# A gated decode block on one core: the whole kernel recorded into one critical section, with a loop on TensorE alone

## The chip, the cores and the metric

The kernel runs on one core of a Trainium2 chip. The metric is the device time of one execution in microseconds (us), lower is better; the time of a kernel is the median over its runs. A core has TensorE (PE; its weight loads are listed as PEld), VectorE (DVE), ScalarE (ACT), GpSimd (POOL) and SyncE (SP), each with an instruction queue of its own, and 16 DMA engines that move data between the chip's memory (HBM) and the core's SBUF.

## The reference, cut to what matters

```python
x = A_x                                     # (4, 1, 512), bf16
mod = silu(c) @ w_mod                       # six parts: sa, ca, ga, sb, cb, gb
h = layernorm(x) * (1 + ca) + sa
q = (h @ wq) as 32 heads of 128             # k_cache, v_cache: (4, 32, 4096, 128)
o = softmax(q . k_cache * 128**-0.5) . v_cache
x = x + ga * (o @ wo)
h = layernorm(x) * (1 + cb) + sb
z = gelu(h @ w_in); z1, z2 = halves of 896
g = w_sp * layernorm(z2) + b_sp             # S is 1: two scalars
out = x + gb * ((z1 * g) @ w_out)
```

The two caches have 134 MB each. They are read once; everything else is small.

## The kernel before, in words

The work is cut into 32 quads. A quad is one batch entry `b` and one group `g` of four heads; quad `i` is `(g, b) = (i // 4, i % 4)`. Its K is one 4 MB load into one of two buffers named `kt` (128 partitions, four heads by 32 parts of the sequence), its V another into one of two named `vt`; both are issued by SP, in the order K of the next quad, `wo_g` (the 512 KB of the output weights of a group, at the first quad of each group), V of this quad (lines 429 to 446). An issue waits until the buffer it writes is free. A load carries 32 KB packets, eight on each of the 16 DMA engines. Ahead of the quads SP loads `w_mod` and `wq` into the two `vt` buffers; the last K and V are cut into parts, and `wo_l`, `win` and `wout` follow them.

For each quad:

- `scores(i, half)`: VectorE multiplies half of K by the query in place (L276); TensorE then adds up the products, 16 matmuls against the identity `ident`, into `s_ps` (L281).
- `fold` (L290) adds eight columns; `softmax` takes the maximum over a head, ScalarE the exponentials (L311), VectorE writes them masked by head into `P4` (L314).
- `values(i - 1)`: 32 matmuls of `P4` with V (L341), and `zsum` the sums of the exponentials; ScalarE copies the result to `osb` (L347).
- `diagonal(i - 2)` picks the right head's rows with `sel` (L354, float32), `project(i - 2)` divides by the sums into `oT` (L375).
- `apply(i - 2)`, at the fourth quad of a group: 16 small matmuls rearrange `oT` (L391), VectorE copies to `oP` (L397), and 16 matmuls with `wo_g` add to `attn_ps` (L400).

In iteration `i` TensorE does diagonal, both halves of scores, values and apply, in this order. Before the loop over quads stand the modulation, the first layernorm and the queries `qbc` (L215 to L266); behind it the second layernorm, the gated MLP and the output (L474 to L545). The whole program is unrolled on all five engines. The order on each engine is that of the text (`tc.manual_schedule()`); the framework (Tile) allots buffers and semaphores and places the waits. Probabilities `P4` and maxima `mx` have three buffers, `wo_g`, `oT` and `oP` two.

Of the kernel before, what the change touches and what calls it, by code (L numbers as in the profile page):

```python
# [8 lines left out]
BF16 = mybir.dt.bfloat16  # L9
# [3 lines left out]
AX = mybir.AxisListType  # L13


@with_exitstack
def kernel(
# [16 lines left out]
    nc = tc.nc  # L34
    ctx.enter_context(tc.manual_schedule())
# [12 lines left out]
    EL = HT * DH  # L48
    DC = 8
    assert J == 4 and DH == P and SK % R == 0 and HT * DC == 512 and FH % P == 0  # L50
    att_scale = float(DH) ** -0.5
    LN_EPS = 1e-5

    consts = ctx.enter_context(tc.tile_pool(name="consts", bufs=1))
    persist = ctx.enter_context(tc.tile_pool(name="persist", bufs=1))
    kvp = ctx.enter_context(tc.tile_pool(name="kv", bufs=1))
    wk = ctx.enter_context(tc.tile_pool(name="work", bufs=1))

    rows = persist.tile([2 * B, D], BF16, name="rows")
    nc.scalar.dma_start(out=rows[0:B], in_=c)
    nc.scalar.dma_start(out=rows[B:2 * B], in_=A_x.rearrange("b s d -> (b s) d"))
    nc.scalar.preload_act_table_set("natural_log_exp_and_others")
    wb_t = persist.tile([1, 2], BF16, name="wb_t")
    nc.gpsimd.dma_start(out=wb_t[:, 0:1], in_=B_w_sp[0:1, 0:1])
    nc.gpsimd.dma_start(out=wb_t[:, 1:2], in_=B_b_sp.rearrange("(a b) -> a b", b=1))


    def vslot(cols):  # L70
        return kvp.tile([P, cols], BF16, name="vt", bufs=2)

    wm = vslot(J * 6 * D)
    nc.sync.dma_start(out=wm, in_=w_mod.rearrange("(p j) n -> p (j n)", j=J))
    wm = wm.rearrange("p (j n) -> p j n", j=J)
    GW = NH * DH
    wq = vslot(J * G * GW)
    nc.sync.dma_start(out=wq, in_=A_wq.rearrange("(p j) n -> p (j n)", j=J))  # L78
    wq = wq.rearrange("p (j n) -> p j n", j=J)

    quads = [(g, b) for g in range(G) for b in range(B)]

    def kv_view(cache, i):
        g, b = quads[i]
        return cache[b, g * NH:(g + 1) * NH].rearrange("h (s n) d -> (h s) (n d)", s=R)

    def load(cache, i, tag, parts):
        t = kvp.tile([P, NT * DH], BF16, name=tag, bufs=2)
        a = 0
        for part in parts:  # L90
            b = a + NT * DH // part
            nc.sync.dma_start(out=t[:, a:b], in_=kv_view(cache, i)[:, a:b])  # L92
            a = b
        return t.rearrange("p (n d) -> p n d", d=DH)

    def load_k(i):
        return load(A_k_cache, i, "kt", (2, 2) if i == len(quads) - 1 else (1,))

    def load_v(i):
        return load(A_v_cache, i, "vt", (2, 4, 8, 16, 16) if i == len(quads) - 1 else (1,))  # L100

    NQ = len(quads)


    ident = consts.tile([P, P], BF16, name="ident")
    make_identity(nc, ident)
    ones_b = consts.tile([1, P], BF16, name="ones_b")
    nc.vector.memset(ones_b, 1.0)
    ones_f = consts.tile([P, P], F32, name="ones_f")
    nc.vector.memset(ones_f, 1.0)  # L110

    sel = consts.tile([P, 32], F32, name="sel")
    nc.vector.tensor_reduce(
        out=sel, in_=ident.rearrange("p (t m) -> p m t", m=32), axis=AX.X, op=ALU.add,
    )
    mean_d = consts.tile([P, P], F32, name="mean_d")
    nc.vector.memset(mean_d, 1.0 / D)
    mean_f = consts.tile([P, P], F32, name="mean_f")
    nc.vector.memset(mean_f, 1.0 / FH)
    eps = consts.tile([P, 1], F32, name="eps")  # L120
    nc.vector.memset(eps, LN_EPS)
    wide = consts.tile([P, 4 * P], BF16, name="wide")
    nc.gpsimd.memset(wide, 0.0)
    busy_ps = [None]

    def keep_busy(n):

        if busy_ps[0] is None:
            busy_ps[0] = psum_s.tile([P, 4 * P], F32, name="big", bufs=2)
        for _ in range(n):  # L130
            nc.tensor.matmul(busy_ps[0], lhsT=ident, rhs=wide, start=True, stop=True)

    NB = 3

    mask4 = consts.tile([P, NH], F32, name="mask4")
    nc.gpsimd.memset(mask4, 0.0)
    for hl in range(NH):
        nc.gpsimd.memset(mask4[hl * R:(hl + 1) * R, hl:hl + 1], 1.0)
    P4s, mxs = [], []
    for i in range(NB):  # L140
        t = consts.tile([P, NT + 4, NH], BF16, name=f"P4_{i}")
        nc.gpsimd.memset(t, 0.0)
        P4s.append(t)
        t = consts.tile([P, R], F32, name=f"mx_{i}")
        nc.gpsimd.memset(t, 0.0)
        mxs.append(t)
# [4 lines left out]
    def ln_stats(pool, psum, buf, ones, n, name, meanwhile=None):  # L151

        nc.vector.tensor_tensor(out=buf[:, 1], in0=buf[:, 0], in1=buf[:, 0], op=ALU.mult)
        ps = psum.tile([P, 2, n, B], F32, name="small", bufs=1)
        nc.tensor.matmul(
            ps.rearrange("p s j b -> p (s j b)"), lhsT=ones,
            rhs=buf.rearrange("p s j b -> p (s j b)"), start=True, stop=True,
        )
        if meanwhile is not None:
            meanwhile()  # L160
        st = pool.tile([P, 2, B], F32, name=f"st_{name}")
        nc.vector.tensor_reduce(
            out=st, in_=ps.rearrange("p s j b -> p s b j"), axis=AX.X, op=ALU.add,
        )
        msq = pool.tile([P, B], F32, name=f"msq_{name}")
        nc.vector.tensor_tensor(out=msq, in0=st[:, 0], in1=st[:, 0], op=ALU.mult)
        var = pool.tile([P, B], F32, name=f"var_{name}")
        nc.vector.tensor_tensor(out=var, in0=st[:, 1], in1=msq, op=ALU.subtract)
        rstd = pool.tile([P, B], F32, name=f"rstd_{name}")
        nc.scalar.activation(out=rstd, in_=var, func=AF.Ln, bias=eps)  # L170
        nc.scalar.activation(out=rstd, in_=rstd, func=AF.Exp, scale=-0.5)
        return st[:, 0], rstd


    modT = persist.tile([P, 6, J, B], F32, name="modT")
    qbc = persist.tile([P, B, G, DH], BF16, name="qbc")
    x1b = persist.tile([P, 2, J, B], F32, name="x1b")
    wbf = persist.tile([P, 2], F32, name="wbf")
    xcT = persist.tile([P, J, 2 * B], F32, name="xcT")
    cT, x4T = xcT[:, :, 0:B], xcT[:, :, B:2 * B]  # L180
    xT = persist.tile([P, J, B], F32, name="xT")


    gwb = persist.tile([P, J, 3, B], F32, name="gwb")
    sT = persist.tile([P, J, B], BF16, name="sT")
    hbc = persist.tile([P, J, B, R], BF16, name="hbc")
    psum_acc = ctx.enter_context(
        tc.tile_pool(name="psum_acc", bufs=1, space=bass.MemoryType.PSUM)
    )
    attn_ps = psum_acc.tile([P, J, B], F32, name="attn_ps")  # L190
    psum_s = ctx.enter_context(
        tc.tile_pool(name="psum_s", bufs=1, space=bass.MemoryType.PSUM)
    )

    def mod_part(oc):
        ps = psum_s.tile([P, J, B], F32, name="small", bufs=1)
        for jo in range(J):
            c0 = oc * D + (jo if oc < 2 else jo * P)
            cols = slice(c0, c0 + (P - 1) * J + 1, J) if oc < 2 else slice(c0, c0 + P)
            for j in range(J):  # L200
                nc.tensor.matmul(
                    ps[:, jo, :], lhsT=wm[:, j, cols],
                    rhs=sT[:, j, :], start=(j == 0), stop=(j == J - 1),
                )
        if oc in (1, 4):
            nc.vector.tensor_scalar_add(out=modT[:, oc], in0=ps, scalar1=1.0)
        else:
            nc.vector.tensor_copy(out=modT[:, oc], in_=ps)

    def query(b, g0, n, qp):  # L210

        for j in range(J):
            wv = wq[:, j, :].rearrange("p (g h d) -> p g h d", h=NH, d=DH)
            for hl in range(NH):
                nc.tensor.matmul(  # L215
                    qp[hl * R:(hl + 1) * R, 0:n], lhsT=hbc[:, j, b, :],
                    rhs=wv[:, g0:g0 + n, hl, :],
                    start=(j == 0), stop=(j == J - 1),
                    tile_position=(0, hl * R),
                )  # L220

    with tc.tile_pool(name="pre", bufs=1) as pre:
        xc_ps = psum_s.tile([P, J, 2 * B], F32, name="small", bufs=1)
        for j in range(J):
            nc.tensor.matmul(
                xc_ps[:, j, :], lhsT=rows[:, j::J],
                rhs=ident[0:2 * B, 0:2 * B], start=True, stop=True,
            )
# [24 lines left out]
        for oc in range(2, 6):  # L253
            mod_part(oc)
# [321 lines left out]
```

## Time and profile before

| | before |
|---|---|
| median of 3 runs | 667.79 us (667.62 to 667.85) |
| span of the profiled execution (first to last instruction) | 665.5 us; the page lists no other time for it |
| PE, DVE, ACT, POOL busy | 415.7, 402.6, 41.3, 4.7 us |
| PE instructions | 3024 weight loads and 3024 matmuls |
| moved from HBM | 282.73 MB, 425 GB/s over the span |
| granted TensorE clock, mean | 0.771 |
| scores matmul L281, VectorE product L276 | 457 ns x1024, 4420 ns x64 |
| K, V: issue to landing, median | 26.0, 33.7 us |

In the profile's slices the span is cut into 40 equal parts of 16.6 us, and a digit gives tenths of a part in which an engine was busy (9: 90% or more). A DMA queue is a stream of packets from one source: q1 holds the loads that SP issues, q8 packets of TensorE's program. A row of instructions gives line, engine, operation, destination and sources, the size of the operation and how often it ran; a figure in brackets behind `<-` is the idle time before it and what ended that.

### The profile page before, as it was taken

What the parts mean: (1) busy time and instruction counts of PE and PEld (TensorE: products, weight loads), DVE (VectorE), ACT (ScalarE), POOL (GpSimd) and SP (SyncE); (2) the same over time, 40 slices, a digit from 0 to 9 for tenths busy, and PEclk for the clock granted to TensorE, in tenths of its full rate; (3) what the DMA queues carried; (4) which work ended last, traced back from release to release, by engine and by line L of the source; (5) the groups of instructions that cost most, each with busy time, mean ns of one, the idle gap of its engine ahead of it and who ended that gap; (6) DMA issues with size and microseconds to landing.
All of it is one profiled execution on the core that took longest, in us unless ns stands there. A gap on an engine that the chain in (4) does not pass through costs nothing.

```text
span 665.5 us, 6939 instructions
## 1 busy us (share of the span) xinstructions
PE 415.7 (62%) x3024; PEld 204.6 (31%) x3024; DVE 402.6 (61%) x475; ACT 41.3 (6%) x115; POOL 4.7 (1%) x21
## 2 busy tenths in 40 slices
PE   2557776655677655676555477654657655657775
PEld 2223333222333322233222233232223322223334
DVE  2166776675556576547666456666555666655762
ACT  1200000000000000000000000000000000000002
POOL 2000000000000000000000000000000000000000
PEclk9977777668887667887667788676888766888795
DMA  9999999999999999999999999999999999999995
GB/s 379 439 425 427 437 439 424 429 438 434 427 428 441 428 428 434 435 426 434 433 436 424 436 435 430 423 439 435 428 431 435 433 430 432 437 426 435 428 417 236
DMA packets 12749, 283.17 MB, mean 426 GB/s; under 512 B 1448, under 2 KB 1968, under 8 KB 4016
## 3 DMA queue, kind: packets, MB, share of 16 engines
q1 hardware_dynamic: 12640, 282.73, 98.9%
q8 instruction: 23, 0.38, 0.2%
q14 instruction: 6, 0.05, 0.0%
q0 software_dynamic: 64, 0.00, 0.0%
q10 hardware_dynamic: 16, 0.01, 0.0%
HBM read 282.73 MB, written 0.00 MB: 425 GB/s over the span
## 4 chain that ended last, share of the span: by engine, by line
DMA 62%; PE 24%; DVE 12%; issue 0%; SPq 0%; ACT 0%; DVEq 0%
DMA kt<-in_A_k_cache_dram 58%; PE s_ps L281 24%; DVE kt L276 11%; DMA vt<-in_A_v_cache_dram 3%; DMA wout_437<-in_B_w_out_dram 1%; PE big L341 0%; DVE S L290 0%; ACT E L311 0%; SPq L92 0%; DVE P_1_109 L314 0%; DVE P_0_105 L314 0%; PE y_ps L522 0%; DVE nm L308 0%; DVE mT L300 0%; SPq L78 0%
## 5 line engine op out<-in xcount | busy, mean ns | idle before, releaser
L281 PE MATMUL s_ps<-kt,ident 128*128 128x512 bf16 x1024 | 293.5, 457 | 185.5 <-DVE kt L276 185.5
L276 DVE TENSOR_TENSOR kt<-kt,qbc 128x8192 bf16<-128x8192 bf16 x64 | 282.7, 4420 | 82.9 <-DMA kt<-in_A_k_cache_dram 82.9
L281 PEld LDWEIGHTS <-ident 128*128 128x128 bf16 x1024 | 116.4, 114 | 351.1 <-issue 229.8
L290 DVE TENSOR_REDUCE S<-s_ps 128x64 f32<-128x512 f32 x64 | 44.3, 692 | 125.5 <-PE s_ps L281 125.5
L354 PE MATMUL zo_ps<-sel,osb 128*128 128x4 f32 x248 | 33.2, 257 | 26.6 <-ACT osb L347 26.6
L311 ACT ACTIVATE E<-S,nm 128x128 f32<-128x128 f32 x32 | 12.8, 401 | 563.4 <-DVE nm L308 563.4
L354 PEld LDWEIGHTS zo_ps<-sel,osb 128*128 128x128 f32 x248 | 30.6, 194 | 38.4 <-ACT osb L347 38.4
L341 PE MATMUL big<-vt,P_0_105 128*32 128x512 bf16 x352 | 21.0, 380 | 1.5 <-DMA vt<-in_A_v_cache_dram 1.5
L341 PE MATMUL big<-vt,P_1_109 128*32 128x512 bf16 x320 | 19.1, 380 | 0.0
L341 PE MATMUL big<-vt,P_2_113 128*32 128x512 bf16 x320 | 19.1, 380 | 0.0
L347 ACT COPY osb<-big 128x512 f32<-128x512 f32 x31 | 17.6, 566 | 20.0 <-PE big L341 20.0
L215 PE MATMUL big<-vt,hbc 128*32 128x512 bf16 x128 | 9.6, 471 | 5.2 <-DMA vt<-in_A_wq_dram 5.2
L314 DVE TENSOR_TENSOR P_1_109<-E,mask_99 128x512 bf16<-128x512 f32 x11 | 7.6, 692 | 6.8 <-ACT E L311 6.8
L314 DVE TENSOR_TENSOR P_0_105<-E,mask_99 128x512 bf16<-128x512 f32 x11 | 7.6, 692 | 6.7 <-ACT E L311 6.7
L341 PEld LDWEIGHTS <-P_0_105 128*32 128x32 bf16 x352 | 8.4, 96 | 8.9 <-DMA vt<-in_A_v_cache_dram 1.6
L314 DVE TENSOR_TENSOR P_2_113<-E,mask_99 128x512 bf16<-128x512 f32 x10 | 6.9, 692 | 6.2 <-ACT E L311 6.2
L400 PE MATMUL attn_ps<-oP,wo_g 128*128 128x4 bf16 x112 | 3.8, 164 | 10.6 <-DVE oP L397 10.6
L341 PEld LDWEIGHTS <-P_1_109 128*32 128x32 bf16 x320 | 7.6, 96 | 6.7
L341 PEld LDWEIGHTS <-P_2_113 128*32 128x32 bf16 x320 | 7.6, 96 | 6.7
L375 DVE TENSOR_TENSOR oT<-zo_ps,rz 128x4 bf16<-128x4 f32 x32 | 5.4, 168 | 7.1 <-PE zo_ps L363 6.0
L215 PEld LDWEIGHTS <-hbc 128*32 128x32 bf16 x128 | 4.4, 114 | 10.3 <-issue 8.4
L308 DVE STREAM_TRANSPOSE nm<-hb 128x32 f32<-128x32 f32 x32 | 6.8, 212 | 1.1
(221 smaller groups left out, 131.1 us busy)
## 6 DMA issues: line engine op xcount, KB each, us to landing
kt<-in_A_k_cache_dram SPq DMA_DIRECT2D x31, 4096.0 KB, 26.0
vt<-in_A_v_cache_dram SPq DMA_DIRECT2D x31, 4096.0 KB, 33.7
vt<-in_A_wq_dram SPq DMA_DIRECT2D x1, 4096.0 KB, 20.4
kt<-in_A_k_cache_dram SPq DMA_DIRECT2D x2, 2048.0 KB, 24.8
wo_g<-in_A_wo_dram SPq DMA_DIRECT2D x7, 512.0 KB, 26.5
vt<-in_w_mod_dram SPq DMA_DIRECT2D x1, 3072.0 KB, 9.8
vt<-in_A_v_cache_dram SPq DMA_DIRECT2D x1, 2048.0 KB, 17.8
win_434<-in_B_w_in_dram SPq DMA_DIRECT2D x1, 1344.0 KB
```

What stands on the lines that cost most here:

```text
L215: nc.tensor.matmul(qp[hl * R:(hl + 1) * R, 0:n], lhsT=hbc[:, j, b, :], rhs=wv[:, g0:g0 + n, hl, :], start=(j == 0), stop=(j == J - 1), til ...
L276: nc.vector.tensor_tensor(out=kt, in0=kt, in1=q[:, None, :].to_broadcast([P, HT, DH]), op=ALU.mult,)
L281: nc.tensor.matmul(ps, lhsT=ident, rhs=kt[:, :, cc * DC:(cc + 1) * DC], start=(cc == 0), stop=(cc == DH // DC - 1),)
L290: nc.vector.tensor_reduce(out=st["S", i][:, half * HT:(half + 1) * HT], in_=st.pop(("s", i, half)), axis=AX.X, op=ALU.add,)
L308: nc.vector.transpose(out=nm, in_=hb)
L311: nc.scalar.activation(out=E, in_=S, func=AF.Exp, bias=nm[:, 0:1], scale=att_scale, accum_out=rs,)
L314: nc.vector.tensor_tensor(out=P4[:, 0:NT, :], in0=E[:, :, None].to_broadcast([P, NT, NH]), in1=mask4[:, None, :].to_broadcast([P, NT, NH]) ...
L341: nc.tensor.matmul(po[32 * t:32 * t + 32], lhsT=P4[:, n0:n0 + 8, :], rhs=st["v", i][:, n0:n0 + 4, :], start=(u == 0), stop=(u == NU - 1), ...
L347: nc.scalar.copy(out=osb, in_=po)
L354: nc.tensor.matmul(st["o", i], lhsT=osb[:, n, :], rhs=sel[:, NH * n:NH * n + NH], start=(n == 0), stop=(n == 3),)
L375: nc.vector.tensor_tensor(out=oT[:, :, b], in0=st.pop(("o", i)), in1=rz, op=ALU.mult,)
L400: nc.tensor.matmul(attn_ps[:, jo, :], lhsT=(wo_g[:, hl] if g < G - 1 else wo_l[hl // 2][:, hl % 2])[:, jo * P:(jo + 1) * P], rhs=oT[:, hl, :],
```

## The change: what it does

- The kernel no longer leaves waits and semaphores to Tile. Each operation is recorded in a `Program` with the regions it reads and writes; `order` finds, for each, which operations of other engines (and which loads) it must wait for, and leaves out those that an earlier wait covers. `run` then emits all engines' instructions inside one `tc.tile_critical()`.
- TensorE's part of quads 2 to 29 is emitted once, for four quads, inside `pe.Fori(0, 7)`; all other engines are still unrolled. What the loop waits for has semaphores of its own (`pe_...`), which TensorE lowers by the pass's count at the end of each pass.
- So that passes are alike, all buffers go by `i % 2`: `P4`, `mx` and the score tiles have two buffers, `wo_g`, `oT` and `oP` one. `wo_g` is loaded at the third quad of a group, between K and V. `attn_ps` is cleared by a matmul with zeros ahead of the loop, and all its matmuls add.
- Outside the tail a matmul is one recorded instruction that brings its weights along (`mm`); in the tail those with `wo_l`, `win` and `wout` are a weight load and a matmul with waits of their own (`mm2`). A semaphore is raised only by operations marked `done`.
- The two one-element loads of `w_sp` and `b_sp` go out from ScalarE's queue instead of GpSimd's; the identity is made by two recorded instructions.

```diff
+class Program:
...
+    def run(self, alloc, passes, engines):
+        self.order()
...
+        for name, lst in self.by_eng.items():
+            if name != "PE":
+                for op in lst:
...
+                    emit(op, engines[name], plain(op))
+        pe = engines["PE"]
+        seen = [o for o in self.by_eng["PE"] if o.passno is None]
+        first = loops[0][0].pos
+        for op in seen:
+            if op.pos < first:
+                emit(op, pe, plain(op))
+        with pe.Fori(0, passes):
+            for op, w in zip(loops[0], norm):
+                emit(op, pe, w.items())
+            for s in sorted(own):
+                if step[s]:
+                    pe.sem_inc(sems[s], -step[s])
+        for op in seen:
+            if op.pos > first:
+                emit(op, pe, [(s, v - passes * step.get(s, 0)) for s, v in plain(op)])
...
-    ctx.enter_context(tc.manual_schedule())
...
-        t = kvp.tile([P, NT * DH], BF16, name=tag, bufs=2)
...
+    kt = tile2([P, NT * DH], BF16, "kt")
+    vt = tile2([P, NT * DH], BF16, "vt")
...
-    NB = 3
+    P4s = tile2([P, NT + 4, NH], BF16, "P4_")
+    mxs = tile2([P, R], F32, "mx_")
...
+    wo_g = sb.tile([P, NH, D], BF16, name="wo_g")
...
+    def mm(out, lhsT, rhs, start, stop, done=False, **kw):
+        prog.add(
+            "PE", lambda e: e.matmul(out, lhsT=lhsT, rhs=rhs, start=start, stop=stop, **kw),
+            [lhsT, rhs], [out], done=done,
+        )
+    def mm2(out, lhsT, rhs, start, stop, done=False):
+        prog.add("PE", lambda e: e.ldweights(lhsT), [lhsT], [], done=False)
+        moving(out, lhsT, rhs, start, stop, done)
...
+    mm(cut(attn_b, J * B), ident, wide[:, 0:J * B], True, True, skip_group_check=True)
...
+    PASSES = (NQ - 4) // B
...
     for i in range(NQ):
+        prog.passno = (i - 2) // B if 2 <= i < 2 + B * PASSES else None
+        g, b = divmod(i, B)
         if i + 1 < NQ:
-            st["k", i + 1] = load_k(i + 1)
-        if quads[i][1] == 0:
-            g = quads[i][0]
-            if g < G - 1:
-                st["wo", g] = wk.tile([P, NH, D], BF16, name="wo_g", bufs=2)
-                nc.sync.dma_start(out=st["wo", g], in_=wo_w[g])
-        st["v", i] = load_v(i)
+            load_k(i + 1)
+        if b == 2 and g < G - 1:
+            load_sp("pe_wo", wo_g, wo_w[g])
+        load_v(i)
...
+    with tc.tile_critical():
+        sems = {}
+        def alloc(name):
+            sems[name] = tc.alloc_semaphore(name)
+            return sems[name]
+        prog.run(alloc, PASSES, {
+            "PE": nc.tensor, "DVE": nc.vector, "ACT": nc.scalar, "POOL": nc.gpsimd, "SP": nc.sync,
+        })
+        nc.sync.wait_ge(sems["out"], 16)
```

## The prediction

> **What bounds the kernel now.** I read the slices of the page first, then the queues, the chain, the windows at the end, the timeline, and last the trace's own list of DMA packets.
>
> ```profile
> PE   2557776655677655676555477654657655657775
> DMA  9999999999999999999999999999999999999995
> q1 hardware_dynamic: 12640, 282.73, 98.9%
> q8 instruction: 23, 0.38, 0.2%
> DMA 62%; PE 24%; DVE 12%; issue 0%; SPq 0%; ACT 0%; DVEq 0%
> ```
>
> The 16 DMA engines are busy in every slice but the last, and queue q1 alone fills 98.9% of them: 282.73 MB must come in. TensorE (PE) is at 62% and waits. So the span is set by when the slowest DMA engine has moved its sixteenth, plus a start of about 1.9 us (first packet) and the last arithmetic. Compute can only matter if it lets the queue run dry, or if it moves bytes. The second small line, q8, is TensorE's program being fetched: 23 packets of 16 KB, by the same 16 engines.
>
> ```profile
> core 0: us, PE busy (x) PEld busy (x) DVE busy (x) ACT busy (x) POOL busy (x), PEclk, DMA share, GB/s
> 600.00:655.00 55.00, 40.93 (x403) 22.09 (x401) 32.26 (x43) 3.12 (x9) 0.00 (x0) 0.81 1.00 424
> ...
> 656.00:657.00 1.00, 0.06 (x1) 0.00 (x0) 0.77 (x5) 0.29 (x1) 0.00 (x0) 0.50 0.67 260
> 657.00:658.00 1.00, 0.19 (x6) 0.22 (x7) 0.35 (x2) 0.95 (x3) 0.00 (x0) 0.50 0.58 235
> ...
> 659.00:660.00 1.00, 1.00 (x27) 0.97 (x25) 0.19 (x1) 0.41 (x2) 0.00 (x0) 0.50 0.48 193
> 660.00:661.00 1.00, 0.90 (x20) 0.76 (x20) 0.73 (x5) 0.99 (x1) 0.00 (x0) 0.50 0.16 61
> ```
>
> (One-microsecond windows; the DMA share is the last column but one.) The engines do not stop together: about half are done at 656 us, the other half work on until 660.6 us. The packet list says why. Every load ends with a 4-byte packet on each of the 16 engines. For the first load these 16 lie within 0.63 us; after the first program fetch (18.4 us) one engine is late and the spread is 1.86 us; it steps to 3.28 at the fetch of 253.5 us and to 4.7 at that of 503.2 us, and is 4.9 us for the last K load. One step, 1.23 us, is what a fetch costs the engine that makes it. At the end seven engines stand within 1.2 us and nine are 3.0 to 4.9 us behind. Following packets from end to start (the gaps are -4 to -2 ns), the fetches go round eight engines: the same engine comes again after eight fetches at six of the eight places. So 23 fetches are nearly 3 on each of eight engines, 3 x 1.23 = 3.7 us on the slowest, and a load has landed only when the slowest has.
>
> ```profile
> 45.07 0.33 SPq L92 DMA_DIRECT2D kt<-in_A_k_cache_dram  x1
> ...
> 62.14 0.33 SPq L92 DMA_DIRECT2D kt<-in_A_k_cache_dram  x1
> ...
> 79.22 0.33 SPq L92 DMA_DIRECT2D kt<-in_A_k_cache_dram  x1
> ```
>
> Near the start, where the data is ahead, a quad takes 17.1 us of compute (45.07, 62.14, 79.22). Later, K issues between 174.13 and 332.05 us make 157.9 us for 8 quads, 19.7 us each, set by DMA. Compute has 2.6 us a quad to spare, 10.6 us for a pass of four.
>
> ```profile
> 611.91 0.54 PE L400 MATMUL attn_ps<-oP,wo_g 128*128 128x4 bf16 x16 [1.51 <-DVE oP L397]
> ...
> 612.31 1.03 PE L354 MATMUL zo_ps<-sel,osb 128*128 128x4 f32 x8
> ...
> 618.55 1.01 PE L281 MATMUL s_ps<-kt,ident 128*128 128x512 bf16 x2 [5.21 <-DVE kt L276]
> ```
>
> This is the place where the new loop jumps back: after `apply` (L400), before `diagonal` (L354). TensorE then idles 5.2 us, from 613.34 to 618.55, for VectorE's product.
>
> **The change, part by part.**
>
> *Program fetches.* TensorE executes 6048 instructions (3024 loads, 3024 matmuls), 23.6 blocks of 256; a block is 16 KB, 23 fetches: one for each block entered. By the built program the new kernel stores 674 instructions ahead of the loop (a float32 matmul counted as two loads and two matmuls, as the 248 records of L354 for its 124 calls show), 664 in it, 790 behind it: 2128, 8.3 blocks, executed as 674 + 7 x 664 + 790 = 6112. No row shows a jump back on TensorE. If the body (41.5 KB) stays where it is held, only 8 blocks are entered for the first time: 8 fetches, one on each of eight engines instead of three, 2 x 1.23 = -2.46 us. If every jump back fetches anew: the loop lies over blocks 2.8 to 5.4, four of them; a jump fetches its target and the next, and each of three crossings one more, 5; 6 x 5 + 8 = 38, nearly 5 an engine, +2.46 us. If an engine is tied to a block's number, five engines make 7, +4.9 us. I take -2.46: eight places of 16 KB in strict rotation look like a memory of 128 KB in which 41.5 KB fit. This is the weakest step, and both ends stay in the range.
>
> [...]
>
> *The jump itself.* The stall per jump is between 0 and 6.5 us: the nearest row is the small load of A_x, issued at 1.33 us and released at 7.81 us among big packets. I take 3; the 5.2 us of idle TensorE above hide it, and beyond that the 10.6 us of a pass. Without the cover it would be 6 x 3 = 18 us. The five semaphore subtractions and the branch are hidden there too.
>
> *Fused matmuls.* Outside the tail, weights and matmul are one instruction with one wait, so the first `ident` load of each half (0.10 us) follows VectorE instead of preceding it: 0.2 us a quad, inside the 2.6 us. In the tail the `wo_l`, `win` and `wout` loads keep their own instruction: nothing.
>
> *wo_g* (512 KB, seven loads) has one buffer instead of two, moves from the first quad of a group to the third, past two V and two K issues, and waits for the previous group's `apply`; the V load stands behind it on SP. `apply` ends at 612.45 where V went out at 610.35, so V goes out some 2.5 us later. V takes 33.7 us from issue to landing, of which 9.7 are its own transfer: 24 us of queue cover it. Bare, it would cost 7 x 2.5 = 17.5 us. The other V, K and tail loads wait for the same events as before.
>
> *Two buffers instead of three* for the probabilities, maxima and scores: `softmax(i)` must now wait for `values(i-2)`, which stands on TensorE before `scores(i)`, for which it waits anyway. Nothing. The zeroing matmul for the accumulator and the two 2-byte loads, moved from POOL to ScalarE's queue (0.3 to 0.7 us each, ahead of a table load of 1.28 us that is needed only at 8.11), are hidden by the wait for K (31.29) and for `rows` (7.81).
>
> *Start and end.* A handshake is added ahead of the first load: between 0 and 0.7 us (the opening barrier, SP waiting 0.7), I take 0.2, since only SP's own signal is awaited. At the end all engines report once more: between 0 and 0.8 us (SP's closing waits, 0.6 for two), I take 0.4.
>
> Sum against the profiled execution: 665.5 - 2.46 + 0.2 + 0.4 = 663.6 us span. The page gives no other time for that execution; the median of the runs, 667.79, is 2.3 above its span, and I keep that: 665.9 us. The whole stream and the arithmetic behind its last landings shift together, so the gain reaches the end.
>
> **The rivals.** *Refetched (slower).* The jump finds nothing held and 38 fetches replace 23: 665.5 + 2.46 + 0.6 + 2.3 = 670.9; tied to block numbers, 673.3. It decides from 24 fetches on: the handshakes already cost 0.6 us, and three more per pass than now are enough. [...] Against it: the rotation over eight.
>
> *Nothing saved.* As many fetches as now, one for each 256 executed (6112 / 256 = 23.9): only the handshakes, 668.4 us.
>
> *The jump binds.* A stall over about 16 us (5.2 + 10.6) would let the queue run dry, each further microsecond costing six; at 17 us, 665.5 + 6 + 0.6 + 2.3 = 674.4. The 6.5 us row speaks against it.
>
> **How the numbers follow.** Held 0.48, refetched 0.38, nothing saved 0.11, jump binds 0.03. A measurement of this kernel can tell about 0.2%, 1.3 us, from no change: 666.45 to 669.13. Held is faster but for 0.03 (handshakes over 1.1 us); nothing saved is the same but for 0.02. Faster 0.45, same 0.12, slower 0.43. Held alone ranges from 665.2 (no handshake cost, 665.3, less the 0.1 by which runs differ) to 666.8 (1.5 us of handshakes). As both signs hold most of the chance, the range goes from 665.2 to 671.0; outside lie the tied engines and the jump that binds, and a little below.
>
> **What would show it.** Right: about 8 packets on q8, the spread of a load's closing packets near 2.5 us at the end, DMA share falling over 2 us rather than 4.5, first K product at about 31.4 us. Wrong: 30 or more q8 packets, or q8 packets in bunches every 79 us; DMA slices under 9 in the middle; L281 waiting for "issue" after each fourth quad. Handshakes show as a first load later than 0.75 us and more than 1.3 us from the last packet to the span's end.

## The result and the profile after

| | before | after |
|---|---|---|
| median | 667.62 us (667.41 to 667.85, 5 runs) | 670.21 us (670.06 to 670.26, 5 runs) |
| ratio, 95% interval | | 1.0039 (1.0026 to 1.0051) |
| span of the profiled execution | 665.5 us | 668.5 us |
| granted TensorE clock, mean | 0.771 | 0.772 |

The changed kernel is 2.6 us slower: a small loss, but one that the interval keeps apart from nothing. The forecast was 665.9.

First the page's lines: slices, rate, queues, chain.

```profile
PE   2557776665576755577655657756557675556784
DMA  9999999999999999999999999999999999999995
DMA packets 12674, 282.92 MB, mean 423 GB/s; under 512 B 1388, under 2 KB 1908, under 8 KB 3956
q1 hardware_dynamic: 12640, 282.73, 98.7%
q8 instruction: 8, 0.13, 0.1%
DMA 63%; PE 24%; DVE 12%; issue 0%; SPq 0%; ACT 0%; DVEq 0%
```

The line with the rate was, before:

```profile
DMA packets 12749, 283.17 MB, mean 426 GB/s; under 512 B 1448, under 2 KB 1968, under 8 KB 4016
```

The step on which the forecast was built came true: TensorE's program is fetched with 8 packets, not 23. They start at 18.8, 33.6, 68.6, 99.9 and 134.3 us, then none until 632.3, 654.3 and 661.3: nothing of it is fetched while the loop goes round. The chain is the old one, and the DMA engines are as full. But the rate is down, 423 GB/s where the kernel before had 426. The same 282.73 MB of q1, with the engines as busy, took longer.

The place of the jump, on TensorE's timeline of the kernel after (columns: start, us, operation; in brackets the idle time ahead and what ended it):

```profile
135.56 0.27 PE L349 MATMUL bank<-oT,ident 128*32 128x4 bf16 x16
137.28 0.55 PE L349 MATMUL bank<-oP,wo_g 128*128 128x4 bf16 x16 [1.46 <-DVE oP L136]
138.54 1.80 PE L349 MATMUL bank<-sel,osb 128*128 128x4 f32 x8 [0.70 <-issue]
144.49 5.78 PE L349 MATMUL bank<-kt,ident 128*128 128x512 bf16 x16 [4.15 <-DVE kt L136]
```

Between `apply` and the next pass's `diagonal` stand 0.70 us of "issue" (the engine waits for nothing that the profile shows): that is the whole price of the jump, and 4.15 us of waiting for VectorE follow it. At the other five jumps it is 0.63 to 0.66 us.

The first issue and the output's issue on SP, in the kernel after:

```profile
0.97 0.39 SPq L141 DMA_DIRECT2D vt<-in_w_mod_dram  x1
665.58 0.36 SPq L727 DMA_DIRECT2D out_dram<-ot  x1
```

Before, these were at 0.75 and 663.16 us. From the output's issue to the span's end it is 668.46 - 665.58 = 2.9 us, and was 665.47 - 663.16 = 2.3. The spans are 3.0 us apart, the medians 2.6: the median stands 1.7 us above this span, where the forecast carried 2.3 over. (In all other runs on record, of both kernels, the two are 1.7 to 1.9 apart, so the execution profiled before was a quick one.) So 0.2 us of span are lost ahead of the first load, 0.6 behind the output, and (665.58 - 663.16) - 0.2 = 2.2 between them, in the stretch where the forecast had a gain of 2.46.

The trace's list of DMA packets shows what became slower. "Closing" are the 4-byte packets with which a load ends on each engine; "last K" is K's last load.

| kernel | plain 32 KB packet, 80 to 620 us, mean ns | fetches | last K: first and last closing packet, us | spread |
|---|---|---|---|---|
| before | 1213.0 | 23 | 637.92, 642.78 | 4.86 |
| after | 1217.1 | 8 | 640.27, 644.68 | 4.41 |

(Plain: without those of over 1300 ns, 21 before and 5 after; each of them starts 0.3 to 1.1 us behind the start of a packet of q8 or q14.) Before, nearly every 32 KB packet takes exactly 1213 ns (6981 of 6989). After, they take 1213 to 1228, on all 16 engines alike. They begin at 1213 (up to 20 us), reach 1214.2 between 35 and 50 us and 1216.7 between 50 and 80. One engine moves some 438 of them between 80 and 620 us: 438 x 4.1 ns = 1.8 us, about 1.9 with those ahead of it. This is most of the loss, and no step of the prediction has it.

What differs for such a packet is where it goes. By the addresses that the built programs give the buffers (bytes in each partition), K and V lay at 121600, 154368, 56064 and 88832 before, all multiples of 256. After they lie at 16512, 49280, 82048 and 114816: each 128 bytes beyond one. In the changed kernel `kt` is the first tile of its only SBUF pool, and what lies ahead of the pool ends at 16512.

### The profile page after: what moved, and what is told of

The parts are those of the page before. It is cut to its first block, busy times and chain, and to the rows that moved or that the text cites. A ratio compares the mean times of both kernels' runs of the same rounds, so it can differ in the third digit from the quotient of the medians.

```text
span 668.5 us, 6869 instructions
## 1 busy us (share of the span) xinstructions
PE 421.6 (63%) x3024; PEld 205.4 (31%) x3025; DVE 402.9 (60%) x475; ACT 41.2 (6%) x115; POOL 3.2 (0%) x17
## 3 DMA queue, kind: packets, MB, share of 16 engines
q1 hardware_dynamic: 12640, 282.73, 98.7%
HBM read 282.73 MB, written 0.00 MB: 423 GB/s over the span
## 4 chain that ended last, share of the span: by engine, by line
DMA 63%; PE 24%; DVE 12%; issue 0%; SPq 0%; ACT 0%; DVEq 0%
DMA kt<-in_A_k_cache_dram 58%; PE bank L349 24%; DVE kt L136 11%; DMA vt<-in_A_v_cache_dram 3%; DMA wout<-in_B_w_out_dram 1%; SPq L141 0%; DVE S L136 0%; DVE P L136 0%; ACT E L136 0%; DVE mx L136 0%; PE bank L360 0%; DVE nm L136 0%; DVE mT L136 0%; DVE hm L136 0%; DVE hb L136 0%
## 5 line engine op out<-in xcount | busy, mean ns | idle before, releaser
L349 PE MATMUL bank<-kt,ident 128*128 128x512 bf16 x1024 | 295.5, 460 | 179.8 <-DVE kt L136 179.8
L349 PEld LDWEIGHTS bank<-kt,ident 128*128 128x128 bf16 x1024 | 114.6, 115 | 348.5 <-DVE kt L136 183.3
L136 DVE TENSOR_REDUCE S<-bank 128x64 f32<-128x512 f32 x64 | 44.3, 692 | 126.4 <-PE bank L349 126.4
L349 PE MATMUL bank<-vt,P 128*32 128x512 bf16 x992 | 59.2, 380 | 0.3 <-DMA vt<-in_A_v_cache_dram 0.3
L349 PE MATMUL bank<-sel,osb 128*128 128x4 f32 x248 | 36.3, 269 | 29.4 <-ACT osb L136 25.0
L349 PEld LDWEIGHTS bank<-sel,osb 128*128 128x128 f32 x248 | 33.6, 210 | 41.9 <-ACT osb L136 36.9
L136 DVE TENSOR_TENSOR P<-E,mask 128x512 bf16<-128x512 f32 x32 | 22.2, 693 | 17.9 <-ACT E L136 17.9
L349 PEld LDWEIGHTS bank<-vt,P 128*32 128x32 bf16 x992 | 23.7, 96 | 21.2 <-DMA vt<-in_A_v_cache_dram 0.4
L136 ACT COPY osb<-bank 128x512 f32<-128x512 f32 x31 | 17.5, 566 | 19.0 <-PE bank L349 19.0
L349 PEld LDWEIGHTS bank<-rs,ones_f 128*128 128x128 f32 x64 | 12.1, 190 | 4.5
## 6 DMA issues: line engine op xcount, KB each, us to landing
vt<-in_A_wq_dram SPq DMA_DIRECT2D x1, 4096.0 KB, 20.5
```

The costliest lines, as they stand in the source:

```text
L136: eng, lambda e: getattr(e, name)(*args, **kw), ins, outs, sem=sem, done=done, after=after,
L349: "PE", lambda e: e.matmul(out, lhsT=lhsT, rhs=rhs, start=start, stop=stop, **kw),
```

## The experiments

Three theories: *address* (the 128 bytes cost the packets 4 ns each), *loop* (something in the repeated passes slows the stream), and *rest* (where the inputs lie in HBM, the loads moved to ScalarE's queue, the critical section's handshakes and waits). All runs are compared with the kernel before in the same session, whose median was 667.53 to 667.60.

**1. The changed kernel with K and V at the addresses of before.**

```diff
+    wo_g = sb.tile([P, NH, D], BF16, name="wo_g")
+    wo_l = tile2([P, NH // 2, D], BF16, "wo_l")
+    qbc = sb.tile([P, B, G, DH], BF16, name="qbc")
...
+    sb.tile([P, 832], BF16, name="pad")
+    vt = tile2([P, NT * DH], BF16, "vt")      # 56064, 88832
+    kt = tile2([P, NT * DH], BF16, "kt")      # 121600, 154368
```

> The changed kernel with its four K and V buffers at the SBUF addresses they have in the kernel before (56064 and on; the changed kernel has them at 16512 and on), nothing else. Address theory: the 32 KB packets of the changed kernel take 1217 ns on the mean instead of 1213 because of where the buffers lie; they go back to 1213, which takes 8064 x 4 ns / 16 = 2.0 us off 670.2: 668.2. Loop theory (TensorE's loop or its program disturbs the DMA engines): packets stay at 1217, 670.2. Third theory (where the inputs lie in HBM, or the loads moved to ScalarE's queue): 670.2 as well.

Measured: 667.16 us (666.78 to 667.35), ratio 0.9994 (0.9985 to 1.0004). Packets 1213.0 ns, 8 fetches. The whole loss is gone.

**2. The changed kernel, everything moved by 128 bytes.**

```diff
+    sb.tile([P, 64], BF16, name="pad")
     kt = tile2([P, NT * DH], BF16, "kt")      # 16640, a multiple of 256
```

> The changed kernel with 128 unused bytes a partition ahead of the K buffers, so that all four begin at a multiple of 256 as in the kernel before (they begin at 128 beyond one now). If the address theory holds and alignment is the reason: packets 1213 ns, 668.2. If the region of SBUF is the reason, or for the other two theories: 1217 ns, 670.2.

Measured: 667.15 us (667.04 to 667.39), ratio 0.9994 (0.9984 to 1.0004), packets 1213.0 ns. The page's lines:

```profile
DMA packets 12674, 282.92 MB, mean 425 GB/s; under 512 B 1388, under 2 KB 1908, under 8 KB 3956
q1 hardware_dynamic: 12640, 282.73, 98.8%
q8 instruction: 8, 0.13, 0.1%
```

Same packets and same fetches as after, and 425 GB/s: one small tile that nobody reads is worth 3.06 us. It isn't the order of the buffers, nor which lies where, but the 128 bytes.

Both runs came out 1.0 us under the 668.2 expected from the 32 KB packets alone. The rest of the 3.06 us is in the traces. The last K's first closing packet is 2.2 us earlier in run 2 than in the kernel after (638.11), its last 2.7 us (642.02, a spread of 3.91), and from there to the output's issue it is 20.5 us instead of 20.9. The smaller packets of the last loads pay too: those of 16 KB take 614.6 ns on the mean in the kernel after and 611.0 in run 2, those of 8 KB 313.7 and 309.0. So the price is about 4 ns for a packet, whether it has 8, 16 or 32 KB.

**3. The seven passes written out, buffers as in the changed kernel.**

```diff
-        with pe.Fori(0, passes):
...
+        for op in self.by_eng["PE"]:
+            if op.pos >= first:
+                emit(op, pe, plain(op))
```

> The changed kernel with TensorE's seven passes written out instead of looped, all waits the same. Loop theory: packets back to 1213 (minus 2.0 us), program fetches back to 23 on eight engines (up to plus 2 us on the slowest): 668 to 670. Address and third theory: packets stay at 1217, fetches 23: 670.5 to 672.2.

Measured: 671.29 us (671.25 to 671.37), ratio 1.0056 (1.0039 to 1.0073); 23 fetches, packets 1217.0 ns, spread of the last K 5.26 us. The loop isn't what slows the packets; taking it out costs another 1.1 us.

**4. The kernel before, with its buffers moved by 128 bytes.**

```diff
+    pad = persist.tile([P, 64], BF16, name="pad")
+    nc.gpsimd.memset(pad, 0.0)
```

> The kernel before with 128 more bytes a partition ahead of its K and V buffers, so that they begin 128 bytes beyond a multiple of 256. Address theory with alignment as the reason: packets 1217, 667.6 + 2.0 = 669.6. All others: 667.6.

Measured: 670.64 us (670.62 to 670.67), ratio 1.0046 (1.0029 to 1.0063), packets 1217.0 ns; again 1.0 us beyond what the 32 KB packets alone give.

```profile
DMA packets 12749, 283.17 MB, mean 423 GB/s; under 512 B 1448, under 2 KB 1968, under 8 KB 4016
q8 instruction: 23, 0.38, 0.2%
```

The kernel before, with nothing of the change in it, falls to the same 423 GB/s and becomes 3.1 us slower. With the second run this settles the cause from both sides.

**5. Written out, and on a multiple of 256** (the edits of 2 and 3 together).

> The changed kernel with its seven passes written out on TensorE and, at the same time, with the K and V buffers moved by 128 bytes, onto a multiple of 256. Address theory (an offset of 128 bytes costs 3.1 us wherever it occurs, the loop is worth 671.29 - 670.21 = 1.1 us): 667.15 + 1.1 = 668.2 us, 23 packets on q8, 32 KB packets of 1213 ns, and about 0.4 to 0.8 us over the kernel before, which is what the handshakes of the critical section cost alone. Rival, the loop is worth its gain only where packets are slow (a fetch cost its engine 1.5 us there and 1.23 us with packets of 1213 ns): 667.4 or less. Rival, the fetches' whole price as in the prediction: 667.15 + 2.46 = 669.6.

Measured: 668.56 us (668.21 to 668.75), ratio 1.0015 (1.0006 to 1.0024); 23 fetches, packets 1213.0 ns, last K's closing packets 638.42 to 643.01. So all of the change but loop and addresses costs 1.0 us: in its trace 0.2 ahead of the first load, 0.6 behind the output's issue (663.60, span 666.47), 0.2 between, which is no more than executions of one kernel differ by. Against run 8 below, of the same session, the loop alone is worth 668.56 - 667.25 = 1.3 us.

**6 and 9. V alone off the multiple, and K alone.** For V alone a second pad of 128 bytes stands between `kt` and `vt`; for K alone, that pad without the first.

```diff
+    sb.tile([P, 64], BF16, name="pad")        # run 6 only
     kt = tile2([P, NT * DH], BF16, "kt")
+    sb.tile([P, 64], BF16, name="pad2")       # both; named pad in run 9
     vt = tile2([P, NT * DH], BF16, "vt")
```

> The changed kernel with the K buffers on a multiple of 256 bytes and the V buffers 128 bytes beyond one. Address theory, each packet paying for its own destination: the V loads are half of the bytes, so half of the 3.1 us, 668.7 us; the 32 KB packets of V in the trace 1217 to 1221 ns, those of K 1213 to 1214. Rival, what counts is how the reads and writes of the compute engines lie against the transfers (any buffer off slows all packets): 670.2 us, or the whole of it from one of the two: 667.2.

> The K buffers stay where the changed kernel has them, 128 bytes beyond a multiple of 256; the V buffers and all that is allotted after them are moved by 128 bytes onto one. With V alone off the multiple the time was 668.36 us (1.2 us above 667.15, plain 32 KB packets 1213.8 ns), with both off 670.21 (3.1 above, 1217.1 ns). If the two prices add, K alone costs the other 1.9 us: 669.0, packets of 1216.3 ns. If it takes a misaligned transfer beside another misaligned one, K alone costs about as much as V alone: 668.3, packets under 1214 ns. If K alone decides (it is what VectorE rewrites in place): 670 or more.

Measured: V alone 668.36 us (ratio 1.0012, 1.0003 to 1.0021), packets 1213.8 ns; K alone 668.04 us (1.0006, 0.9997 to 1.0015), packets 1213.6. Halves would have been 1215. By the packets it is not additive: 0.8 and 0.6 ns, and 4.1 when both are off. The times, 1.2 and 0.9 us above 667.15, add to 2.1 of 3.06; part of them is a wider spread of the closing packets (4.67 with V alone, 4.09 with K alone, 3.91 in run 2).

The packet lists of the two runs show that the price builds up ("on" and "off": on a multiple of 256 or not). The table has the mean of the 32 KB packets, in ns, that start within one microsecond, counted from the middle closing packet of the load ahead (all such loads between 80 and 620 us; in the first 3 us late engines still move the load ahead):

| load | 0 to 1 us | 3 to 4 | 5 to 6 | 7 to 8 | 8 to 9 |
|---|---|---|---|---|---|
| run 6, V (off) | 1213.5 | 1213.8 | 1214.1 | 1214.6 | 1215.3 |
| run 6, K (on) | 1214.7 | 1213.0 | 1213.0 | 1213.0 | 1213.0 |
| run 9, K (off) | 1213.0 | 1213.0 | 1213.2 | 1214.1 | 1215.1 |
| run 9, V (on) | 1215.2 | 1213.1 | 1213.0 | 1213.0 | 1213.0 |

It grows through a load that is off and is gone a few microseconds into one that is on; in the kernel after no K or V load is on, and the mean stays at 1217 once it is there. What builds up, no run shows. It does not follow VectorE, the rival in the expectation of run 6: in the kernel after, packets during which VectorE works throughout take 1217.2 ns, those during which it is idle 1217.0. Run 6 differs from the kernel after, by the multiple of 256, in K alone; the small tiles allotted behind V move with V in both runs, so V is not parted from them.

**7 and 8. Other offsets:** pads of 64 bytes (K at 16576) and 384 bytes (K at 16896, a multiple of 512).

> The changed kernel with its buffers moved by 64 bytes: K at 16576, 192 bytes beyond a multiple of 256. If what counts is being on a multiple of 256 bytes at all, 670.2 us as with 128 bytes, packets near 1217 ns. If a part below 128 bytes adds pieces that a step of 128 does not, slower still, 672 us or more. If the distance to the next multiple sets it (64 bytes instead of 128), between 667.2 and 670.2, about 668.7.

> The changed kernel with its buffers moved by 384 bytes: K at 16896 and all four on a multiple of 512 bytes, where the kernel before and the two fast variants stand on odd multiples of 256. If 256 is the step that counts: 667.15 us, packets of 1213.00 ns. If 512 gains once more: below 666.5 and packets under 1213. If the multiple of 512 is worse (two engines meeting at the same place): above 668.

Measured: 670.28 us (ratio 1.0041, 1.0028 to 1.0055) with packets of 1217.0 ns for 64 bytes; 667.25 us (0.9995, 0.9986 to 1.0004) with 1213.0 for 384. So of the offsets run, those on a multiple of 256 are the quick ones: 192 bytes beyond one cost what 128 cost (670.28 and 670.21 us), and a multiple of 512 gains nothing more (667.25 against 667.15).

**10 and 11. How long a body TensorE holds:** buffers as in run 2, loop bodies of eight quads (three passes, 83 KB) and of twelve (two passes, 124.5 KB).

```diff
-    PASSES = (NQ - 4) // B
+    PQ = 8                                    # run 11: 12
+    PASSES = (NQ - 4) // PQ
...
-        prog.passno = (i - 2) // B if 2 <= i < 2 + B * PASSES else None
+        prog.passno = (i - 2) // PQ if 2 <= i < 2 + PQ * PASSES else None
```

> Buffers on a multiple of 256; the loop has three passes of eight quads (quads 2 to 25) instead of seven of four, and quads 26 to 31 follow written out. The body is 1328 instructions, 83 KB, and the whole program 3456 stored, 13.5 blocks. If what TensorE holds covers 83 KB: 13 or 14 packets on q8 and none from the second pass's start (about 190 us) to its end; by the two measured points (8 fetches 667.15, 23 fetches 668.56, 0.094 us a fetch) 667.7 us. If it holds less than 83 KB (a window of 64 KB or of two blocks): about 24 fetches, 668.6 us. By the prediction's price of 1.23 us for each round of eight engines, 0.154 us a fetch: 668.0.

> As before, with two passes of twelve quads: a body of 1992 instructions, 124.5 KB, 7.8 blocks of 16 KB, in a program of 16.1 blocks. If TensorE holds 128 KB in blocks of 16 KB and the body's eight or nine blocks do not quite fit, the second pass fetches them anew: 24 or 25 packets on q8, 668.6 us. If they fit: 16 or 17 packets and 667.9 us. If the place behind the jump has to wait (the jump stalls the product by several us), more than 669.

Measured, eight quads: 667.26 us (667.13 to 667.42). The body is held: 13 fetches, none between 192.9 and 536.2 us. The five more than in run 2 cost 0.1 us, or nothing against run 8 (667.25), and not the 0.5 to 0.8 that a price for each fetch would give.

```profile
q8 instruction: 13, 0.21, 0.1%
```

Measured, twelve quads: 669.74 us (ratio 1.0033, 1.0021 to 1.0045), 26 fetches, among them 300.2, 305.8 and 312.0 us, behind the one jump back (that of 291.3 us is ahead of it, and run 5 has it too, at 291.2). Queue and chain on the page, then TensorE's timeline there:

```profile
q8 instruction: 26, 0.43, 0.2%
DMA 59%; PE 26%; DVE 13%; issue 2%; ACT 0%; SPq 0%; DVEq 0%
```

```profile
295.02 0.55 PE L350 MATMUL bank<-oP,wo_g 128*128 128x4 bf16 x16 [1.45 <-DVE oP L136]
302.64 1.87 PE L350 MATMUL bank<-sel,osb 128*128 128x4 f32 x8 [7.07 <-issue]
304.37 3.15 PE L350 MATMUL bank<-kt,ident 128*128 128x512 bf16 x7
308.16 6.33 PE L350 MATMUL bank<-kt,ident 128*128 128x512 bf16 x25 [0.64 <-issue]
```

This body isn't held, and the jump that finds nothing costs 7.07 us of TensorE ("issue"), ten times the 0.70 of the loop of four. The stream did not notice. The chain leads through the jump, and the K behind it went out at 314.51 us, 3.3 us later than in the written-out run 5; but the first closing packet of the load at 344 us is at 344.22, and at 344.20 in run 5: the queue covered the delay. The time above run 5 (1.2 us, most of it behind the last K: the last packet of 3 KB or more ends at 662.39, there at 661.00) has more fetches in it and 1.8 us of waiting for `wo_l`, which are 0.2 in runs 5 and 10. What of it causes the 1.2 us is not shown.

The versions on a multiple of 256 with the loop (1, 2, 8 and 10: 667.15 to 667.26) are the quickest, 0.3 to 0.4 us under the kernel before. That is inside the 0.2% that can't be told from no change.

## Why the prediction was wrong

It was wrong on the sign, and the step that failed is one that it did not have: it lists new buffer counts and costs them "nothing", and never asks where the new code puts the buffers that the stream writes. The sum, with what the runs showed for each term:

| step | forecast | measured |
|---|---|---|
| fetches 23 to 8, body held | -2.46 us | 8 fetches, held; worth -1.3 us (runs 5 and 8) |
| jump back, hidden | 3 us each, cost 0 | 0.7 us or less each, hidden |
| handshake ahead of the first load | +0.2 | +0.2 |
| handshake behind the output | +0.4 | +0.6 |
| `wo_g`, fused matmuls, two buffers | 0 | +0.2 together (run 5), within what executions differ by |
| K and V 128 bytes off a multiple of 256 | not in the sum | +3.1 (runs 2 and 4) |

Measured terms: -1.3 + 0.2 + 0.6 + 0.2 + 3.1 = +2.8 against 670.21 - 667.62 = 2.6. Without the last row the change is worth -0.4 us (run 2: 667.15 against 667.55), and the case that the prediction called likeliest would have ended as "same".

*The fetches.* The mechanism was right to the packet, its price was not. The prediction took 1.23 us off for each of two rounds over eight engines. On 15 of the 16 engines this is what happened: in run 2 they close the last K within 2.4 us, where run 5 needs 4.6. The sixteenth closes at 3.9, and a load has landed only then (in the kernel after, the closing packets of a K load start between 611.06 and 614.50 us, and VectorE, idle until then, begins its product at 614.99). The page has another queue of kind "instruction", q14, with six packets of 8 KB; the prediction passed over it, though its own list had nine engines late where eight take the fetches. Three of those six (237.4, 434.5 and 616.9 us) fall on one engine in run 2, as far as packets can be followed from one to the next (for the last of them this is plain, for the others not everywhere). The spread steps from 2.40 to 3.07 after the second and stands at 3.91 after the third. In the kernel after, too, one engine is late alone: 4.41 us, and the other 15 within 2.5. So the sign that was promised, 2.5 us, came on 15 engines and not on the slowest, which is the only one that counts. That a queue of 0.05 MB takes about half of the gain is read from the packets; no run took it away. Run 10 agrees: five more fetches, on engines with time to spare, cost 0.1 us.

*The end.* The other sign, the DMA share falling over 2 us, failed likewise. The one-microsecond windows of the kernel after (the DMA share is the last column but one):

```profile
core 0: us, PE busy (x) PEld busy (x) DVE busy (x) ACT busy (x) POOL busy (x), PEclk, DMA share, GB/s
658.00:659.00 1.00, 0.48 (x2) 0.35 (x2) 0.41 (x3) 0.00 (x0) 0.00 (x0) 0.50 0.97 383
659.00:660.00 1.00, 0.00 (x0) 0.00 (x0) 0.56 (x5) 0.81 (x3) 0.00 (x0) 0.50 0.65 261
660.00:661.00 1.00, 0.79 (x26) 0.87 (x27) 0.16 (x1) 0.97 (x1) 0.00 (x0) 0.50 0.38 152
661.00:662.00 1.00, 1.00 (x33) 0.96 (x32) 0.10 (x1) 0.19 (x1) 0.00 (x0) 0.50 0.15 44
662.00:663.00 1.00, 1.00 (x20) 0.92 (x19) 0.42 (x3) 0.74 (x2) 0.00 (x0) 0.50 0.05 22
```

It falls over about 4 us, but in another shape. Before, a plateau near one half (0.58 from 657 us, 0.48 from 659) showed half of the engines late together; now the share sinks steadily, and its last microsecond (0.05) is less than one engine in sixteen.

*The rival "refetched"* gave 670.9 us, and 670.2 was measured, but it did not happen: there are 8 fetches, not 38, and none in bunches every 79 us. A time that fits a rival is no evidence for it when its own signs are absent. What it supposed does occur with a longer body: in run 11 (124.5 KB) fetches follow the jump at 300.2, 305.8 and 312.0 us, and there are 26 in all for a program of 16.1 blocks. The 6.5 us that the prediction took as the jump's upper end, from a small load among big packets, was near: 7.07. The cover held too: the load behind the jump landed no later than in run 5.

*What TensorE holds.* That the eight engines in rotation tell how much TensorE holds was the prediction's estimate, and no run shows the size itself. The runs bracket it: bodies of 41.5 and 83 KB were repeated without one fetch (none between 134.3 and 632.3 us in the kernel after, none between 192.9 and 536.2 in run 10) and with jumps of 0.7 us or less; the nine blocks that 124.5 KB touch when 674 instructions stand ahead of the loop were not all held (run 11).

*The addresses.* The runs agree on the boundary (1213.0 ns on a multiple of 256, 1217 at 128 and at 192 bytes beyond one) and on a price for the packet and not for its bytes (4.1 ns for 32 KB against the kernel before; 3.6 for 16 KB and 4.7 for 8 KB against run 2). At 192 bytes it is 4.0 ns, no more than at 128. Why a packet pays it, and why the price builds up and is not there in the first 20 us (1213 ns), no run shows.

## What to carry to other kernels

In a kernel that a stream of loads bounds, look up in both built programs at which address the stream's buffers lie, before costing anything else: a rewrite that lets other code allot the tiles can move them (here by 128 bytes beyond a multiple of 256, at 3.1 us), and the diff doesn't show it. A gain on one resource of sixteen counts only as far as the slowest goes (run 2: 15 engines within 2.4 us, the sixteenth at 3.9), so list everything that lands on it, small queues too. And when a measured time fits a rival, look for the rival's signs before believing it.

## What the runs showed of the hardware

- In these kernels a 32 KB packet into SBUF takes 1213.0 ns when K and V start at a multiple of 256 bytes (runs 1, 2, 5 and 8) and 1217 when both start 128 or 192 bytes beyond one (runs 3, 4 and 7): 3.0 to 3.1 us of 667, at 128 bytes in both kernels. Packets of 16 and 8 KB pay about the same (3.6 and 4.7 ns).
- The price builds up over a load that is off (1213.0 to 1215.1 ns in run 9), and is gone a few microseconds into one that is on (1213.1 from 3 us): with only K or only V off the mean is 1213.6 to 1213.8. In the first 20 us of the kernel after, packets take 1213 even when off.
- TensorE repeated a body of 41.5 KB (the kernel after) or 83 KB (run 10) without fetching it again, and a jump back cost it 0.7 us or less. At 124.5 KB (run 11) fetches follow the jump, 26 in all, and it cost 7.07 us while the DMA engines were full.
